# A convolution and sixteen experts in one kernel: one group's convolution sums move from TensorE to VectorE, with the loads, scatters and logits around them

## The chip, the cores and the metric

One core of a Trainium2 chip runs the whole program. The time is device microseconds of one execution, and the figure for a kernel is the median of its runs. Engines are named as in the profile: PE is TensorE (PEld its weight loads), DVE is VectorE, ACT is ScalarE, POOL is GpSimd, and SP issues most DMAs.

## What is computed

```python
# x: 8 x 2880 x 192, weight_gen: 8 x 2880 x 8 x 7
w = softmax(weight_gen, axis=-1)                         # 7 taps for each token and head
out = einsum('bshk,bskhg->bshg', w, x_unf)               # causal convolution, 8 heads x 24 channels
x = out.reshape(23040, 192)
g_logits = x @ w_group                                   # 4 groups of 4 experts
g_idx = argmax(g_logits);  g_w = softmax(g_logits)[g_idx]
e_logits = x @ w_expert[g_idx]
e_idx = argmax(e_logits);  e_w = softmax(e_logits)[e_idx]
h = relu(x @ w1[g_idx, e_idx])                           # 192 -> 1024
y = g_w * e_w * (h @ w2[g_idx, e_idx])                   # 1024 -> 192
```

Each token goes through one expert of sixteen. All of it is in 32-bit floats.

## The kernel before

The 23,040 tokens lie as 128 partitions x 180. They are taken in 15 groups of 12 columns (1,536 tokens), each in two half groups of 6.

**The front** (`front`, L656) makes, group by group, what the experts need. `load_group` (L229) loads the taps (`wt`) and the tokens (`xin`, in two parts; buffers for two groups). `softmax` (L252) is DVE with one exponential on ACT. `conv` (L274) forms the seven products of a half group on DVE (`product`, L279, `pr`, three buffers) and sums them in one of two ways. For the first `TURNED` half groups PE adds them up: nine transposes of 128 x 128 for each product accumulate in three PSUM banks (L319), and the sum comes out turned. For the others DVE adds with six additions (L298). `route` (L351) makes logits on PE (`logits`, L357: eight products for four columns, in 32 columns of the array), then the choice of expert, and the position of each token's row (`posi`, L500). A turned sum gives its logits directly and is turned back by `back` (L369, three transposes and a copy on ACT each). Another sum is first turned by `forward` (L378), three transposes and a copy into `xT` for every two columns, with logits after every second. POOL then scatters the rows of 12 x 128 tokens to the place of their expert in device memory (`scatters`, L519, L533).

**The visits.** A visit takes up to 256 rows of one expert through both products (`gemm1` L881, `gemm2` L908, LAG = 2 units behind; a visit has four units). `table` (L547) lists at the end of each round, from counts, which block and which expert each visit has; ROUNDS (L19) says that the first round ends with group 2 and has 10 small visits (128 rows, weights used as they are loaded), that round 1 has 4 visits of 256 rows, round 2 has 5, and so on for each further group. The large ones split w1 into a high and a low part (`split`, L802, cast on ACT and subtraction on DVE, both recorded as L806, L809 and L824), and so do their rows (`xlo`). The low parts of a third of w1 are made once, by `halves` (L619), with stores to device memory. `finish` (L924) scales and evacuates the result on ACT (L928), POOL sends it (`send`, L936).

**What sets the order.** PE, ACT, DVE and SP run in the order in which the program emits. `blocks` (L961) emits the visits, unit by unit, and between them steps the front (`fill`, `step`, `move`) by clocks that it keeps itself (`run`, L203). Loads are put on a list by `ask` (L977) and emitted by `pump` (L964), which stops at the first that is not ready. `ask_w` asks for w1, part 3 is w2, part 0 is the rows (`xb`, L770), which wait on the chip for the scatters. `warm` (L209) emits fillers (L214) that keep PE active. Small visits have three buffers of w1 (`wa`), four of w2 (`wc`); large ones two of raw w1. Small transposed tiles share one bank (`tp`).

```python
TURNED = 10                                                          # L25
if state["slots"] or 2 * g + n >= TURNED:                            # L288, else PE adds
if n in (2, 8) and 1 <= g < ENDS[-1] - 1:                            # L668
if end and n + 3 < n1 and (plain(n + 3) or plain(n + 1)):            # L1074
```

Of the kernel before, what the change touches and what calls it, by code (L numbers as in the profile page):

```python
# [21 lines left out]
HURRY = 12  # L22
EVERY = {}
WHOLE = (99,) * 11 + (3, 0, 0)
TURNED = 10  # L25


class Slot:
# [4 lines left out]
def conv_moe_kernel(ctx: ExitStack, tc: tile.TileContext, x, wgen, w_group, w_expert, w1, w2, out):  # L33
# [169 lines left out]
    def run(eng, cost, *deps):  # L203
        clk[eng] = max([clk[eng]] + [d + HOP for d in deps]) + cost
        return clk[eng]
# [23 lines left out]
    def load_group(g, parts=(0, 1)):  # L229
        if parts == (1,):  # L230
            s0, mid = g * SG, (SG + HALO) // 2
            nc.sync.dma_start(out=grp[g].xin[:, mid:, :], in_=xv[:, s0 - HALO + mid:s0 + SG, :])
            return
        o = grp[g] = Slot()
        o.ahead, o.chunks = False, 0
        s0 = g * SG
        o.wt = cv.tile([P, SG * H, K], F32, name="wt")
        nc.sync.dma_start(out=o.wt.rearrange("p a k -> p (a k)"), in_=wv[:, s0:s0 + SG, :])
        o.xin = cv.tile([P, SG + HALO, D], F32, name="xin")
        if s0 == 0:  # L240
            nc.gpsimd.memset(o.xin[:, 0:HALO, :], 0.0)
            nc.sync.dma_start(out=o.xin[:, HALO:, :], in_=xv[:, 0:SG, :])
            for b in range(B):
                lo, hi = b * PB, (b + 1) * PB
                nc.sync.dma_start(out=o.xin[lo + 1:hi, 0:HALO, :], in_=xv[lo:hi - 1, S - HALO:S, :])
        else:
            end = SG + HALO if 1 in parts else (SG + HALO) // 2
            nc.sync.dma_start(out=o.xin[:, 0:end, :], in_=xv[:, s0 - HALO:s0 - HALO + end, :])
# [102 lines left out]
    def route(g, o):  # L351
# [5 lines left out]
        def logits(s4, xTs):  # L357
            for u in range(2):
                for j in range(4):
                    xT, turned = xTs[j // 2]  # L360
                    if turned:
                        v, c = (((0, 0), (1, 1)), ((3, 1), (4, 2)))[j % 2][u]
                    else:
                        v, c = u * (1 + j % 2), (j % 2, 2)[u]
                    nc.tensor.matmul(  # L365
                        lt[j * LW:(j + 1) * LW, s4 // 4, :], lhsT=wr[:, v, :], rhs=xT[:, c, :],
                        start=u == 0, stop=u == 1, tile_position=(0, j * LW))
# [10 lines left out]
        def forward():  # L378
            xTs = []
            for s2 in range(0, SG, 2):  # L380
                n, i = s2 // SC, s2 % SC // 2
                if o.chunks <= n:
                    yield Chunk(o, n + 1)
                row = xrow[n][:, s2 % SC:s2 % SC + 2, :]
                if i == 0:
                    rem = rt.tile([P, SC, HP], F32, name="rem")
                    nc.scalar.copy(out=rem, in_=xrow[n][:, :, P:D])
                    txT = run("act", 0.4, clk["dve"])
                    yield NEXT
                ttp = run("pe", 0.35, txT)  # L390
                tp = ps_t.tile([P, 3, P], F32, name="tp")
                for u in range(2):
                    nc.tensor.transpose(out=tp[:, u, :], in_=row[:, u, 0:P], identity=ident)  # L393
                nc.tensor.transpose(out=tp[:, 2, :], in_=rem[:, s2 % SC:s2 % SC + 2, :].rearrange("p s d -> p (s d)"), identity=ident)
                if len(xTs) == 2:
                    run("pe", 0.5, txT)
                    logits(s2 - 4, xTs)
                    xTs = []
                xT = rt.tile([P, 3, P], F32, name="xT", bufs=2)
                nc.scalar.copy(out=xT, in_=tp)  # L400
                txT = run("act", 0.48, ttp)
                xTs.append((xT, False))
                yield NEXT
            run("pe", 0.5, txT)
            logits(SG - 4, xTs)

        turned = 2 * g < TURNED
        if turned:
# [110 lines left out]
    def scatters(g, xrow, pi):  # L519
        for s in range(SG):  # L520
            run("pool", 1.28, clk["dve"])
            scatter_row(pi[:, s:s + 1], xrow[s // SC][:, s % SC, :], round_of(g))
            yield NEXT
        if g >= MAIN and g + 1 in ENDS[:-1]:
            arrive_all(round_of(g))

# [129 lines left out]
    def front():  # L656
        side, routes = [], []
        load_group(0)
        set_up()
        load_group(1)  # L660
        yield from softmax(0)
        for g in range(ENDS[-1]):
            o = grp[g]
            routes.append([route(g, o), None])
            state["urgent"] = g == FIRST
            for n, c in enumerate(conv(g, o)):
                yield c
                if n in (2, 8) and 1 <= g < ENDS[-1] - 1:  # L668
                    load_group(g + 1, (n // 8,))
                if n >= (12 if state["slots"] else 4) and not o.ahead and g + 1 < ENDS[-1]:  # L670
                    o.ahead = True
                    side.append([softmax(g + 1), None])
                if g == FIRST - 1 and n == 4:
                    slow.append([halves(), None])
                    yield from move(slow, slow[0], 1)
                if g >= FIRST and n % 2 == 0 and not state["urgent"]:
                    for q in list(slow):
                        yield from move(slow, q, 2)
                if not state["urgent"]:
                    for q in side[:1]:  # L680
                        yield from move(side, q, 3)
                for q in spread[:1]:
                    yield from move(spread, q, 1)
                if routes:
                    yield from move(routes, routes[0], HURRY if FIRST <= g < MAIN else 3 if g < FIRST else 8 if g in ENDS else 2)
            yield from finish_all(side)
            yield from finish_all(routes, 1)
            yield from finish_all(spread, 1)
        yield from finish_all(spread)
        yield from finish_all(routes)  # L690
# [270 lines left out]
    def blocks(n0, n1, paced):  # L961
        want, jobs = [], []

        def pump(upto=None):  # L964
            for a in list(want):
# [8 lines left out]
                want.remove(a)  # L974
                load(*a)

        def ask(n, part):  # L977
            if n < n1:
                want.append((n, part))

        def ask_x(n):
# [44 lines left out]
        if n0 + 2 < n1 and plain(n0 + 2):  # L1026
            ask_w(n0 + 2)
            ask(n0 + 2, 3)
        for n in range(n0, min(n0 + 3, n1)):
            ask(n, 0)  # L1030
        if n0 + 2 < n1 and not plain(n0 + 2) and (whole(n0 + 2) or whole(n0 + 1)):
# [15 lines left out]
        for i in range(len(units) + LAG):  # L1047
            if i < len(units):
                n, j, u = units[i]
                gemm1(cur, u)  # L1050
                queue.append((cur, u))
                if i + NU - u < len(units):
                    if u == 0:
                        pump(units[i + NU][0])
                        nxt = block(i + NU)
                        prep_d(nxt)
                    if u == 1:
                        prep_x(nxt, (i + NU) // NU)
                if u == NU - 1 and i + 1 < len(units):
                    cur = nxt  # L1060
            asks = []
            if i >= LAG:
                b, u = queue.pop(0)
                gemm2(b, u)
                if u == NU - 1:
                    finish(b)
                    if i - LAG + 1 < len(units) and units[i - LAG + 1][0] != units[i - LAG][0]:
                        asks.append(units[i - LAG][0] + 3)
            if i < len(units):
                n, j, u = units[i]  # L1070
                nb = blocks_of(n)
                at = j * NU + u
                end = at == nb * NU - 1
                if end and n + 3 < n1 and (plain(n + 3) or plain(n + 1)):  # L1074
                    ask_w(n + 3)
                did = 0
                for job in list(jobs):
                    m, part, h = job
                    if m > n + 2 or (part == 3 and (m > n + 1 or at < LAG)):
                        continue  # L1080
                    must = end and m == n + 1
                    if not must and (did >= 1 or (m, part) in want or not ready(m)):
                        continue
                    jobs.remove(job)
                    work_split(job)
                    did += 1
                state["unit"] += 1
            flush()
            if paced:
                fill(clk["pe"] + AHEAD[0 if cur.plain else 1 if cur.o.whole else 2])  # L1090
            for a in asks:
                ask_x(a)
            pump()
# [40 lines left out]
```

## Time and profile before

| | us |
|---|---|
| median of 3 runs | 1240.73 (1240.4 to 1241.85) |
| the profiled execution, its own time | 1243.13 |
| its span | 1241.5 |
| PE busy in the span | 1190.0 |
| DVE busy | 922.6 |
| ACT busy | 662.1 |
| POOL busy | 428.0 |

The profile is of one execution, and sums made from its rows compare with its own time. A timeline row says when a group of like instructions starts, how long it is on record and how long its engine stood before it, with the instruction that ended this. PE's rows overlap, so what one costs is the distance to the next row's start. One product in 32-bit floats is two records in PE's rows, a transpose is one.

### The profile page before, as it was taken

Reading aid. Unit: us, or ns where it says so; the run is one execution under the profiler, and the core shown is the slowest. Engines: PE = TensorE matmul, PEld = TensorE weight load, DVE = VectorE, ACT = ScalarE, POOL = GpSimd, SP = SyncE. Lnnn points to the kernel's source line nnn. Section 1 sums busy time; section 2 is a strip of 40 time slices with the busy share of each in tenths; the row PEclk is TensorE's granted clock in tenths of the full one; section 3 lists DMA queues with packets and bytes.
Section 4 is the critical chain, followed back from the end, with each engine's and each line's share of the span. In section 5 each row is a group of like instructions: output and inputs, shape, how many; then the busy total and the mean of one; then the engine's idle time right before and its main releaser. Section 6 shows DMA issues by size and latency. Waiting matters only on the chain.

```text
span 1241.5 us, 26600 instructions
## 1 busy us (share of the span) xinstructions
PE 1190.0 (96%) x9456; PEld 1162.9 (94%) x9456; DVE 922.6 (74%) x1582; ACT 662.1 (53%) x1242; POOL 428.0 (34%) x412
## 2 busy tenths in 40 slices
PE   5998899899999999999999999999998999999995
PEld 5887899899999999999999999999998999999995
DVE  8887678698989898898899889961255776777500
ACT  1223333455565555555656565555665777777531
POOL 3062424151626253433424342444154112211111
PEclk9999999899999999999999999999998999999998
DMA  4448988888877888797969786868569777776891
GB/s 150 137 137 245 271 289 263 251 248 268 245 259 232 274 237 265 214 295 222 282 204 301 218 279 206 238 199 259 179 188 300 226 224 232 221 224 199 233 261 43
DMA packets 181677, 286.08 MB, mean 230 GB/s; under 512 B 16084, under 2 KB 141775, under 8 KB 181280
## 3 DMA queue, kind: packets, MB, share of 16 engines
q1 hardware_dynamic: 162304, 245.09, 65.8%
q0 software_dynamic: 19232, 39.22, 9.6%
q8 instruction: 76, 1.25, 0.4%
q14 instruction: 65, 0.53, 0.1%
HBM read 240.89 MB, written 44.33 MB: 230 GB/s over the span
## 4 chain that ended last, share of the span: by engine, by line
PE 67%; issue 20%; DVE 4%; POOL 4%; DMA 3%; ACT 1%; SPq 0%; POOLq 0%; DVEq 0%; ACTq 0%
PE py L919 27%; PE ph L892 27%; POOL out L936 3%; PE pl L365 2%; PE ph L319 1%; PE py L214 1%; DVE pr L280 1%; PE py L319 1%; PE tpx L319 1%; PE tpx L868 1%; PE tpx L869 1%; PE tp L393 1%; DMA raw<-in_moe_w 1%; PE tp L374 1%; DMA wc<-in_moe_w 1%
## 5 line engine op out<-in xcount | busy, mean ns | idle before, releaser
L892 PE MATMUL ph<-xh,wa 128*128 128x256 f32 x2064 | 459.7, 299 | 0.0
L936 POOL DMA_INDIRECT out<-xb x190 | 207.2, 1090 | 657.3 <-ACT xb L928 407.5
L919 PE MATMUL py<-wc,hh 128*128 128x192 f32 x2240 | 417.7, 327 | 9.8 <-ACT xb L928 9.8
L919 PEld LDWEIGHTS py<-wc,hh 128*128 128x128 f32 x2240 | 359.9, 191 | 10.2 <-ACT xb L928 10.2
L892 PE MATMUL ph<-xlo,wa 128*128 128x256 f32 x1376 | 359.4, 283 | 0.0
L892 PEld LDWEIGHTS ph<-xh,wa 128*128 128x128 f32 x2064 | 351.0, 191 | 7.4 <-issue 5.9
L898 ACT ACTIVATE hh<-ph 128x512 f32<-128x512 f32 (+1 forms) x316 | 173.2, 548 | 317.2 <-PE ph L892 317.2
L892 PEld LDWEIGHTS ph<-xlo,wa 128*128 128x128 f32 x1376 | 262.5, 191 | 0.0
L280 DVE TENSOR_TENSOR pr<-xin,wt 128x1152 f32<-128x1152 f32 x190 | 253.6, 1351 | 6.2 <-PE tpx L319 6.1
L533 POOL DMA_INDIRECT rows<-xrow,posi x180 | 201.9, 1122 | 133.2 <-DVE posi L500 57.2
L298 DVE TENSOR_TENSOR xrow<-xrow,pr 128x1152 f32<-128x1152 f32 x120 | 162.4, 1353 | 0.6
L824 DVE TENSOR_TENSOR wa<-raw,wa 128x1024 fp32r<-128x1024 f32 x86 | 104.9, 1220 | 71.2 <-ACT wa L806 63.8
L921 PE MATMUL py<-wc,hh 128*128 128x384 f32 x400 | 122.5, 362 | 0.0
L824 DVE SCALAR_TENSOR_TENSOR hl<-ph,hh 128x512 fp32r<-128x512 f32 x100 | 69.1, 691 | 66.8 <-ACT hh L903 66.4
L922 PE MATMUL py<-wc,hl 128*128 128x192 f32 x400 | 100.8, 252 | 0.0
L806 ACT CAST wa<-raw 128x1024 fp32r<-128x1024 f32 x86 | 90.3, 1050 | 6.2 <-DMA raw<-in_moe_w 6.2
L809 ACT CAST wa<-raw 128x1024 fp32r<-128x1024 f32 x86 | 89.5, 1040 | 0.0
L928 ACT ACTIVATE xb<-py,xb 128x192 f32<-128x192 f32 x190 | 71.6, 420 | 27.3 <-PE py L919 21.5
L892 PE MATMUL ph<-xd,wa 96*128 96x128 f32 x576 | 78.8, 281 | 0.5 <-ACT xd L862 0.5
L922 PEld LDWEIGHTS py<-wc,hl 128*128 128x128 f32 x400 | 77.5, 194 | 0.0
L921 PEld LDWEIGHTS py<-wc,hh 128*128 128x128 f32 x400 | 76.2, 190 | 0.0
L892 PEld LDWEIGHTS ph<-xd,wa 96*128 96x128 f32 x576 | 75.1, 198 | 0.8 <-ACT xd L862 0.7
(165 smaller groups left out, 1291.2 us busy)
## 6 DMA issues: line engine op xcount, KB each, us to landing
wc<-in_moe_w SPq DMA_DIRECT2D x79, 768.0 KB
raw<-in_moe_w SPq DMA_DIRECT2D x86, 512.0 KB
raw<-in_moe_w SPq DMA_DIRECT2D x102, 256.0 KB
xin<-in_x SPq DMA_DIRECT2D x26, 864.0 KB
raw<-w1lo SPq DMA_DIRECT2D x86, 256.0 KB
raw<-in_moe_w SPq DMA_DIRECT2D x25, 768.0 KB
xb<-rows SPq DMA_DIRECT2D x86, 194.0 KB
wa<-in_moe_w SPq DMA_DIRECT2D x36, 384.0 KB
```

Source lines behind the costliest of these rows:

```text
L280: nc.vector.tensor_tensor(out=dst, in0=o.xin[:, c0 + k:c0 + k + SC, :].rearrange("p s (h g) -> p s h g", g=HG), in1=w4[:, c0:c0 + SC, :, k ...
L298: nc.vector.tensor_tensor(out=acc, in0=acc, in1=prs[k - 2], op=ALU.add)
L533: written_once(nc.gpsimd.indirect_dma_start(out=rows[:, :], out_offset=bass.IndirectOffsetOnAxis(ap=idx, axis=0), in_=src, in_offset=None, ...
L806: nc.scalar.copy(out=o.wa[:, 0, :], in_=o.raw[0])
L809: nc.scalar.copy(out=o.wa[:, 2, :], in_=o.raw[1])
L824: f(*a, **k)
L892: nc.tensor.matmul(ph[:, v, :], lhsT=w[:, f0:f0 + P], rhs=rhs, start=i == 0, stop=i == len(terms) - 1)
L898: nc.scalar.activation(out=hh, in_=ph, func=AF.Relu)
L919: nc.tensor.matmul(b.py[t][:, 0:D], lhsT=hh[:, v, c], rhs=wc[0][:, f, :], start=f == 0, stop=f == NFT - 1)
L921: nc.tensor.matmul(b.py[t], lhsT=hh[:, v, c], rhs=wc[f // 4][:, f % 4].rearrange("p l d -> p (l d)"), start=f == 0, stop=False)
L922: nc.tensor.matmul(b.py[t][:, 0:D], lhsT=hl[:, v, c], rhs=wc[f // 4][:, f % 4, 0, :], start=False, stop=f == NFT - 1)
L936: ins = nc.gpsimd.indirect_dma_start(out=out[:, :], out_offset=bass.IndirectOffsetOnAxis(ap=b.x.bitcast(I32)[:, t, D + 1:D + 2], axis=0), ...
```

## The change

- `TURNED` is 8: group 4's two half groups are summed on DVE, and group 4 takes the way of `forward`. Groups 0 to 3 stay.
- In `forward`, groups before `BATCH` = 13 keep all six turned tiles (four in buffers of `hl`, two in `xT`) and make their 24 logits products in one go.
- `scatters`: up to group 7 the front emits two scatters for each unit, not one.
- `front`: the first part of a group's load is emitted at the first step of the group before, not the third, for groups 2 to 4.
- `blocks`: the fourth visit's w2 is asked for at the start; w1 of the first two large visits is asked for one visit earlier; nothing is asked for twice.

```diff
-TURNED = 10
+TURNED = 8
+BATCH = 13
...
-                if len(xTs) == 2:
+                if len(xTs) == 2 and g >= BATCH:
                     run("pe", 0.5, txT)
                     logits(s2 - 4, xTs)
                     xTs = []
-                xT = rt.tile([P, 3, P], F32, name="xT", bufs=2)
+                if g < BATCH and s2 < 8:
+                    xT = wp.tile([P, 3, P], F32, name="hl", bufs=4)
+                else:
+                    xT = rt.tile([P, 3, P], F32, name="xT", bufs=2)
...
-            run("pe", 0.5, txT)
-            logits(SG - 4, xTs)
+            run("pe", 0.25 * len(xTs), txT)
+            for q in range(len(xTs) // 2):
+                logits(SG - 2 * len(xTs) + 4 * q, xTs[2 * q:2 * q + 2])
...
             scatter_row(pi[:, s:s + 1], xrow[s // SC][:, s % SC, :], round_of(g))
-            yield NEXT
+            if g >= 8 or s % 2:
+                yield NEXT
...
-                if n in (2, 8) and 1 <= g < ENDS[-1] - 1:
-                    load_group(g + 1, (n // 8,))
+                at = (0 if g < FIRST + 2 else 2, 8)
+                if n in at and 1 <= g < ENDS[-1] - 1:
+                    load_group(g + 1, (at.index(n),))
...
+        asked = set()
+
         def ask(n, part):
-            if n < n1:
+            if n < n1 and (n, part) not in asked:
+                asked.add((n, part))
                 want.append((n, part))
...
             ask(n0 + 2, 3)
+            if n0 + 3 < n1 and plain(n0 + 3):
+                ask(n0 + 3, 3)
...
-                if end and n + 3 < n1 and (plain(n + 3) or plain(n + 1)):
+                if end and n + 3 < n1 and plain(n + 3):
                     ask_w(n + 3)
+                if end and n + 4 < n1 and plain(n + 2) and not plain(n + 4):
+                    ask_w(n + 4)
```

Three places where the emitted order moves. Lines behind the first edit have other numbers in the changed kernel.

PE at the first visit. `xb_158` are its rows, turned by two transposes; `ident,pr` are accumulating transposes, here the last of group 2, `pl<-hl` its logits. Before:

```order
L214 MATMUL py_1398<-ident 128x128 x9
L319 MATMUL ph_1397<-ident,pr 128x128 x3
...
L214 MATMUL py_1398<-ident 128x128 x11
L365 MATMUL pl<-hl,wr 32x128 x16
...
L860 MATMUL tp<-ident,xb_158 96x128 x2
L892 MATMUL ph_1584<-xd_167,wa 128x128 x4
```

Changed:

```order
L215 MATMUL py_1409<-ident 128x128 x13
L867 MATMUL tp<-ident,xb_158 96x128 x2
L899 MATMUL ph_1492<-xd_167,wa 128x128 x4
L320 MATMUL ph_1408<-ident,pr 128x128 x3
...
L899 MATMUL ph_1519<-xd_167,wa 128x128 x4
...
L215 MATMUL py_1409<-ident 128x128 x14
L366 MATMUL pl<-hl,wr 32x128 x16
```

The first visit's transposes and its first two units now stand ahead of the last 27 accumulating transposes of group 2 and of its logits.

SP before the large visits: `raw_170` and `raw_171` are the two buffers of w1, which visits 10 and 11 use, 12 uses the first again; `xb_160` are visit 10's rows. Before:

```order
L786 DMA raw_170<-in_moe_w 128x1024
...
L770 DMA xb_160<-rows 128x388
...
L786 DMA raw_170<-in_moe_w 128x1024
...
L786 DMA raw_171<-in_moe_w 128x1024
```

Changed:

```order
L793 DMA raw_170<-in_moe_w 128x1024
...
L777 DMA xb_159<-rows 128x194
...
L793 DMA raw_171<-in_moe_w 128x1024
...
L777 DMA xb_160<-rows 128x388
...
L793 DMA raw_170<-in_moe_w 128x1024
```

Visit 11's load stood behind visit 12's; now it stands ahead of visit 10's rows, and visit 10's ahead of visit 9's rows.

DVE at the positions of group 4 (`posi`), with the subtractions of the large visits (`wa<-raw` for w1, `xlo` for the rows). Before, where two `xlo` rows stand ahead of it in the program:

```order
L824 TENSOR_TENSOR wa<-raw_170,wa 128x1024
L824 TENSOR_TENSOR xlo<-tpx,xh_168 128x512
L497 TENSOR_REDUCE pos<-sel 128x12
L500 SCALAR_TENSOR_TENSOR posi<-pos 128x12
L558 TENSOR_TENSOR units<-cnt,per_unit 128x16
```

Changed, with six:

```order
L831 TENSOR_TENSOR wa<-raw_170,wa 128x1024
L831 TENSOR_TENSOR xlo<-tpx,xh_168 128x512
L269 TENSOR_TENSOR wt<-wt,z 128x672
...
L502 TENSOR_REDUCE pos<-sel 128x12
L505 SCALAR_TENSOR_TENSOR posi<-pos 128x12
```

For group 5 the counts are 8 and 12, for group 6 they are 14 and 17, for groups 7 to 13 two or three more than before, and for group 14 one more. The whole of PE's order has 504 accumulating transposes where it had 630, and 310 fillers where it had 325.

## Rows read from the trace of the kernel before

**Rows 1.** The page: busy time of the engines over the span, and from its list of groups the scatters of the front and the additions of the half groups that DVE sums (busy us, mean ns of one, idle before).

```profile
PE 1190.0 (96%) x9456; PEld 1162.9 (94%) x9456; DVE 922.6 (74%) x1582; ACT 662.1 (53%) x1242; POOL 428.0 (34%) x412
...
L533 POOL DMA_INDIRECT rows<-xrow,posi x180 | 201.9, 1122 | 133.2 <-DVE posi L500 57.2
L298 DVE TENSOR_TENSOR xrow<-xrow,pr 128x1152 f32<-128x1152 f32 x120 | 162.4, 1353 | 0.6
```

**Rows 2.** Windows: stretch, its length, then busy time of PE, PEld, DVE, ACT and POOL, granted clock of PE (1 is 2.4 GHz), share of time in which the DMA engines are busy, GB/s.

```profile
101.30:238.70 137.40, 122.74 (x1053) 116.23 (x1051) 98.66 (x190) 50.15 (x116) 39.10 (x34) 0.95 0.86 259
124.00:155.00 31.00, 26.52 (x203) 25.76 (x202) 20.79 (x48) 9.98 (x23) 14.31 (x12) 0.94 0.98 271
155.00:186.00 31.00, 30.01 (x282) 28.67 (x280) 22.55 (x38) 12.22 (x30) 6.96 (x6) 1.00 0.89 291
238.70:832.00 593.30, 593.30 (x4640) 579.59 (x4639) 536.96 (x882) 346.38 (x644) 243.91 (x214) 1.00 0.80 247
```

**Rows 3.** Timelines of PE, ACT, DVE and SP around 131 us, the first hole: start, us, engine, line, operation, count, and in brackets the idle time before with what ended it.

```profile
130.75 1.06 PE L892 MATMUL ph<-xd,wa 96*128 96x128 f32 x8
136.00 0.92 PE L919 MATMUL py<-wc,hh 128*128 128x192 f32 x4 [4.19 <-ACT xb L928]
...
140.27 0.82 PE L919 MATMUL py<-wc,hh 128*128 128x192 f32 x4
...
134.34 0.76 ACT L258 ACTIVATE wt<-wt 128x672 f32<-128x672 f32 x1 [5.83 <-DVE wt L257]
...
132.56 0.85 DVE L255 TENSOR_REDUCE m<-wt 128x96 f32<-128x672 f32 x1 [7.99 <-DMA wt<-in_weight_gen]
...
126.56 0.58 SPq L238 DMA_DIRECT2D wt<-in_weight_gen  x1
```

**Rows 4.** Timelines of PE, ACT and SP around 230 us, the second hole, up to the first product of a large visit (238.75).

```profile
227.92 1.05 PE L892 MATMUL ph<-xd,wa 96*128 96x128 f32 x8
234.57 1.65 PE L919 MATMUL py<-wc,hh 128*128 128x192 f32 x4 [5.59 <-ACT xb L928]
...
238.75 0.77 PE L892 MATMUL ph<-xh,wa 128*128 128x256 f32 x2
...
232.39 1.04 ACT L806 CAST wa<-raw 128x1024 fp32r<-128x1024 f32 x1 [6.17 <-DMA raw<-in_moe_w]
...
224.84 0.35 SPq L786 DMA_DIRECT2D raw<-in_moe_w  x1
```

**Rows 5.** Timeline of PE: two rows of three accumulating transposes each.

```profile
130.10 0.49 PE L319 MATMUL py<-ident,pr 128*128 128x128 f32 x3
130.43 0.49 PE L319 MATMUL tpx<-ident,pr 128*128 128x128 f32 x3
```

**Rows 6.** Timelines of POOL, SP and PE ahead of the first visit: the last scatter of group 1, the load of the first three visits' rows, then PE's fillers, logits, transposes back, and the first visit's transposes and products.

```profile
100.38 1.91 POOL L533 DMA_INDIRECT rows<-xrow,posi  x1 [0.30 <-issue]
...
107.92 3.10 SPq L770 DMA_DIRECT2D xb<-rows  x3
...
103.81 1.15 PE L214 MATMUL py<-ident 128*128 128x128 f32 x9
...
110.56 1.08 PE L365 MATMUL pl<-hl,wr 128*32 128x128 f32 x32
...
112.01 0.55 PE L374 MATMUL tp<-ident,hl 128*128 128x128 f32 x3
...
...
115.36 0.43 PE L860 MATMUL tp<-ident,xb 128*96 128x128 f32 x2 [0.57 <-ACT xrow L375]
116.24 1.99 PE L892 MATMUL ph<-xd,wa 96*128 96x128 f32 x8 [0.46 <-ACT xd L862]
```

**Rows 7.** Timeline of PE: one of the three batches of logits of group 5, between a transpose and the products of a visit.

```profile
267.84 0.27 PE L394 MATMUL tp<-ident,rem 128*128 128x128 f32 x1
268.04 0.64 PE L365 MATMUL pl<-xT,wr 128*32 128x128 f32 x16
268.62 0.50 PE L892 MATMUL ph<-xh,wa 128*128 128x256 f32 x2
```

**Rows 8.** DMA issues from 60 to 260 us: destination and source, queue, count, KB each.

```profile
wc<-in_moe_w SPq DMA_DIRECT2D x15, 768.0 KB
wa<-in_moe_w SPq DMA_DIRECT2D x20, 384.0 KB
xin<-in_x SPq DMA_DIRECT2D x8, 864.0 KB
w1lo<-raw SPq DMA_DIRECT2D x16, 256.0 KB
raw<-in_moe_w SPq DMA_DIRECT2D x14, 256.0 KB
raw<-in_moe_w SPq DMA_DIRECT2D x6, 512.0 KB
...
wt<-in_weight_gen SPq DMA_DIRECT2D x4, 336.0 KB
```

**Rows 9.** Timelines of DVE and PE: the positions of group 4 on DVE, the first use of rows of its round (the tenth large visit) on PE, and that of the next round (the sixteenth).

```profile
245.82 0.17 DVE L500 SCALAR_TENSOR_TENSOR posi<-pos 128x12 int32<-128x12 f32 x1
...
330.20 0.27 PE L868 MATMUL tpx<-ident,xb 128*128 128x128 f32 x1
...
398.38 0.27 PE L868 MATMUL tpx<-ident,xb 128*128 128x128 f32 x1
```

## The prediction

> **What bounds the kernel now.** I read the page's busy table first, then the windows, then the timelines of single engines where TensorE (PE) stands. PE is busy 96% of the span, DVE 74% [rows 1]. By stretch it is sharper: from 238.7 us to 832 us PE is busy 593.3 of 593.3 us, while DVE has 56 us free and the DMA engines a fifth [rows 2]. There every microsecond of PE work is a microsecond of time, and the stretch simply starts later or sooner. Before it, from 101.3 to 238.7 us, PE is busy 122.7 of 137.4 us. That part, where ten visits of 128 tokens run between the accumulating transposes of groups 2 to 4, holds two holes:
>
> - At 130.75 us PE issues a first product that needs 0.9 us, and its next row starts at 136.00. It waited for ScalarE's (ACT) evacuation of the previous visit; ACT stood in front of the exponential of group 4's weights, that for DVE, and DVE for the load of these weights, issued only at 126.56 [rows 3]. After it PE runs at half clock: from 136.00 to 140.27 it takes 4.27 us for what needs 2.52 later. Cost: 4.35 + 1.75 = 6.1 us.
> - At 227.92 us the same, 5.75 us: ACT waits 6.17 us for the weights of the second 256-token visit, which were issued at 224.84, behind those of the third [rows 4]. From 234.57 to 238.75 PE then takes 4.2 us for 1.8 us of products, at half clock again: 2.4 more. Cost: 8.1 us.
>
> **The change part by part.**
>
> *Eight half groups.* 14 products of group 4 are no longer summed on PE: 14 x 9 = 126 transposes at 0.109 us (three start 0.33 us apart [rows 5]): -13.7 us. The order has 310 fillers where it had 325: -1.6. Group 4's way back from the turned layout made PE wait for ACT between its four copies, as the 0.57 us ahead of 115.36 [rows 6]: four such waits, -2; the transposes that take their place stand between other products. DVE gets 12 additions more, 1.35 us each as in its other half groups [rows 1]: 16.2 us. They are covered by the 56 us that DVE has free behind 238.7 us and the 39 us before it [rows 2]; without that cover they would cost up to 16.2.
>
> *Loads sooner.* Group 4's weights are asked for two products earlier and stand before two stores and a load of 512 KB in SP's order. The weights of the first two 256-token visits are asked for one visit earlier, the second's no longer behind the third's (the second excerpt). I take both holes as gone: -6.1 and -8.1. What is late next is the DMA, below. The fourth visit's w2 (768 KB) is put in front of the first visit's rows; at some 300 GB/s that is 2.6 us.
>
> *The first visit stands earlier in PE's order*, before the last 27 transposes, the logits and the way back of group 2 (the first excerpt of the order). But its rows cannot come earlier: the last scatter of group 1 is issued at 100.38, and SP could start the load only at 107.92 [rows 6]. PE reaches the place at about 105.2, where the last 9 fillers end, and stands until about 112 (107.92, the extra load, and some 2 us to land). So the first visit starts 3.4 us sooner than at 115.36, and 9.6 us of work stand behind it that stood ahead (27 x 0.109, 14 fillers 1.5, logits 1.45, 12 transposes 1.3, and 2.4 us of waits for ACT, four of some 0.6): +6.2. Bounds: 4.7 if the rows land as now, 8 if the extra load delays the scatters as well. Half clock behind this wait is in both kernels (at 116.24 eight products are 1.99 us on record, at 130.75 they are 1.06 [rows 3, 6]).
>
> *Logits in one batch.* Eight products in 32 columns take 0.58 us to the next product's start, and the row before them holds PE 0.20 us instead of 0.11 [rows 7]; 24 in one go take 1.45 us (110.56 to 112.01 [rows 6]). Three batches come to about 2.1 us, one to 1.6: 0.5 us for each of groups 5 to 12, -4. Bounds: 0 and -5. The copies into other tiles cost ACT the same.
>
> *Scatters two a unit.* On the chip a scatter already follows the next after 0.30 us of issue [rows 6]; the order only moves sends out from between them. Nothing, as long as the rows are in time (rival below).
>
> *DMA.* Between the first visit's rows and the first 256-token product the new order still has to move what these are sized at [rows 8]: 16 stores and 8 loads of 256 KB for the split weights, 5 x 864 and 2 x 336 KB for groups 3 to 5, 14 x 384 and 7 x 768 KB for visits, 2 x 1,024 KB for the first two large ones, and 4 MB of rows, scatters and results: 28.4 MB. PE has 97 us of work there by the rows above (102.4 us of products before, less 12.0; then 2.4 us of half clock and 4.5 of waits for ACT). At 271 GB/s with a share of 0.98 the bytes need 105 us, at 291 with 0.89, that is 327 at full, 87 [rows 2]. So a wait between 0 and 10 us with what the last visit adds; I take 4, nearer to the faster row, because the small stores that fill 124 to 155 us are done by the half of it.
>
> By the Trainium skill ("DMA: Bandwidth & Descriptors", Specifications) a core's HBM limit is about 358 GB/s. By it, an estimate, the bytes need 79 us and this wait is nothing. No stretch of rows 2 comes near it, so the rows decide.
>
> **Sum**: -13.7 - 1.6 - 2 - 6.1 - 8.1 + 6.2 - 4 + 4 = -25.3 us. The profiled execution took 1243.13 us (span 1241.5), so 1217.8 for such a one; the median of the runs shown is 2.4 us lower, so **1215.5 us**. The first 256-token product would start at about 213 us instead of 238.75.
>
> **Rivals.**
>
> *A, a new hole before the first large visit.* For it: the visits that are left run 6.2 us each without transposes between them, each wants 1.57 MB, and the new order has ACT meet the exponential of group 5's weights before the evacuation that PE needs, not behind it; I find 3 us to spare there. Visit 10's rows queue behind 1 MB of visit 11's weights. Against it: no PE row before waited for these loads. If the DMA runs at 271 GB/s throughout or one hole of the kind of rows 4 (8.1 us) is back, 8 us more: 1224.
>
> *B, the DMA keeps up.* With no wait at all and the rows of the first visit as early as now: 1215.5 - 4 - 1.5 = 1210. For it the 327 GB/s. By the skill's limit above it would be so; no row shows that rate.
>
> *C, rows of a round come late: slower than before.* DVE now makes the positions of group 4 after the low halves of six large visits, not two, and of group 5 after twelve, not eight (third excerpt). Positions to first use were 84 us for group 4 [rows 9]; four visits of 11.4 us (398.38 less 330.20, six visits) come off. What is left, 39 us, must hold 12 scatters (1.12 + 0.30 each: 17 us [rows 1, 6]), their landing (5.6, from 102.3 to 107.9), the load of rows (3) and a unit ahead (3): about 7 to 10 us to spare. If they are late, ACT stands before the copy of these rows, and each such round costs one hole, 8.1 us. Ten rounds have this boundary; it decides from the fourth hole on, and five give 1256. Against it: later groups shift by two to three visits only, and one or two holes leave it at 1224 to 1232.
>
> The Trainium skill speaks for C ("SBUF — State Buffer", Who interferes with whom): a DVE instruction with two inputs in SBUF contends with a GpSimd instruction that reads SBUF, and here twelve such additions are added. If every scatter waited out one of 1.35 us, that would be 16 us more for twelve of them, past what is to spare. The trace hardly agrees: the 180 scatters take 1.12 us in the mean [rows 1], most of them beside a DVE that is busy nine tenths of the time [rows 2].
>
> *D, the change does not do what it says*, both holes stay because the loads stand behind others in the same queues: -25.3 + 14.2 = -11, 1230.
>
> **Chances.** The sum 50%, A 20%, B 15%, D 6%, C with one to three holes 3%, with more 5%, no change from effects that cancel 1%. Range: the likeliest case with its bounds is 1211 to 1220; adding B below, and A and the lower part of D above, gives **1207 to 1230**, which leaves out C, the outer part of D and what lies under B. Faster by over 0.2% (about 2.5 us, what a measurement of this kernel can tell from no change): 93%; within: 2%; slower: 5%.
>
> **What would show it.** Right: 168 rows of accumulating transposes in each bank instead of 210; no row of PE behind an evacuation for over 4 us between the first visit and the first 256-token product; that product at 209 to 216 us; one wait of 5 to 8 us ahead of the first visit's transposes, with half clock behind it; logits in rows of 24 for groups 4 to 12; PE full from there on, and the hole near 949 us, which I leave as it is, about 25 us sooner. Wrong: a wait of ACT for a load of weights or rows of over 3 us in that stretch (A, D), or PE holes behind 250 us at the start of rounds (C).

## The result and the profile after

| | before | changed |
|---|---|---|
| median of 5 runs, us | 1240.88 (1240.40 to 1241.85) | 1221.56 (1217.02 to 1223.24) |
| ratio to before | | 0.9835, interval 0.9814 to 0.9856 |
| the profiled execution, us | 1243.13 | 1217.97 |
| first 256-token product on PE, us | 238.75 | 217.91 |
| PE busy, us | 1190.0 | 1165.7 |

The change saves 1.65%, some 20 us. The runs lie in the forecast range and on the forecast side, but the median is 6 us above the point forecast and only 2.4 from rival A's 1224. The profiled execution happens to be the second fastest, so the spans of the two profiles differ by 25.1 us where the medians differ by 19.3; the experiments below say where its luck lies.

The page after, busy time and the two groups that answer to [rows 1] (busy us, mean ns, idle before):

```profile
PE 1165.7 (96%) x9315; PEld 1144.1 (94%) x9315; DVE 935.0 (77%) x1594; ACT 658.9 (54%) x1238; POOL 439.6 (36%) x412
...
L539 POOL DMA_INDIRECT rows<-xrow,posi x180 | 198.2, 1101 | 136.1 <-DVE posi L505 67.1
L299 DVE TENSOR_TENSOR xrow<-xrow,pr 128x1152 f32<-128x1152 f32 x132 | 178.6, 1353 | 0.6
```

PE has 24.3 us less to do. The 12 additions cost DVE 16.2 us as priced, and the scatters beside them did not get longer: 1.10 us, where they had 1.12. So the contention of DVE and GpSimd that the Trainium skill states ("SBUF — State Buffer", Who interferes with whom), which spoke for rival C, has no size in the scatters here. POOL's 190 sends of results did get longer, from 1.09 to 1.17 us in the mean, but not by these additions: e11 below, which has none of them, has 1.18.

Windows after, answering to [rows 2] (stretch, length, busy time of PE, PEld, DVE, ACT and POOL, PE's granted clock, DMA share, GB/s):

```profile
101.30:217.90 116.60, 102.32 (x845) 97.79 (x844) 82.55 (x158) 43.95 (x101) 35.59 (x34) 0.94 0.94 280
198.00:204.00 6.00, 0.23 (x3) 0.11 (x2) 5.93 (x5) 1.33 (x2) 4.52 (x5) 0.85 1.04 351
204.00:210.00 6.00, 6.00 (x28) 5.99 (x29) 1.43 (x2) 2.13 (x5) 4.74 (x5) 0.58 1.05 293
217.90:832.00 614.10, 614.10 (x4873) 605.68 (x4872) 562.40 (x926) 362.23 (x675) 261.88 (x220) 1.00 0.84 252
```

PE is full from its first 256-token product up to 832 us, as before. Ahead of that product the DMA engines are now nearly full (0.94, with 0.86 before; a share a little over 1 in a short stretch reads as full), and from 198 to 204 us PE is busy for 0.23 of 6 us. After that its clock is near half (0.58) for 6 us.

Timeline of PE after, ahead of the first visit ([rows 6] before), with half clock behind the wait:

```profile
103.42 1.58 PE L215 MATMUL py<-ident 128*128 128x128 f32 x13
109.99 0.60 PE L867 MATMUL tp<-ident,xb 128*96 128x128 f32 x2 [4.98 <-DMA xb<-rows]
111.05 2.08 PE L899 MATMUL ph<-xd,wa 96*128 96x128 f32 x8 [0.46 <-ACT xd L869]
112.91 0.85 PE L320 MATMUL ph<-ident,pr 128*128 128x128 f32 x3
...
120.30 1.75 PE L215 MATMUL py<-ident 128*128 128x128 f32 x14 [1.23 <-ACT xlo L326]
121.97 1.08 PE L366 MATMUL pl<-hl,wr 128*32 128x128 f32 x32
```

PE stands 5 us for the rows, where 6.8 were forecast (105.2 to 112); they come 2 us sooner (109.99), and the logits of group 2 come behind it. The transposes at 112.91 go at half clock (0.85 on record, where three take 0.49 at full).

Timelines of PE and SP after, from the loads of visit 10's weights (`raw`) to the first 256-token product; the last small visit's rows are the `xb` of 193.17:

```profile
197.06 1.06 PE L899 MATMUL ph<-xd,wa 96*128 96x128 f32 x8
203.89 0.66 PE L867 MATMUL tp<-ident,xb 128*96 128x128 f32 x2 [5.77 <-DMA xb<-rows]
205.63 1.91 PE L899 MATMUL ph<-xd,wa 96*128 96x128 f32 x8
...
217.91 0.48 PE L899 MATMUL ph<-xh,wa 128*128 128x256 f32 x2
...
189.89 0.35 SPq L793 DMA_DIRECT2D raw<-in_moe_w  x1
190.43 0.57 SPq L796 DMA_DIRECT2D raw<-in_moe_w  x1
191.19 0.50 SPq L796 DMA_DIRECT2D raw<-w1lo  x1
191.73 0.58 SPq L233 DMA_DIRECT2D xin<-in_x  x1
193.17 0.33 SPq L777 DMA_DIRECT2D xb<-rows  x1
```

The two old holes (131 and 229 us, [rows 3, 4]) are gone, and one like them is new. The rows, 97 KB, stand behind 1 MB of weights and 864 KB of tokens and land some 10 us after their issue. It costs 5.8 us and about 2.5 of half clock: 8.3.

The logits of one group after ([rows 7] before):

```profile
308.28 1.08 PE L366 MATMUL pl<-hl,wr 128*32 128x128 f32 x32
309.17 0.62 PE L366 MATMUL pl<-xT,wr 128*32 128x128 f32 x16
```

24 products take 0.89 and 0.55 us to the next row. Before, a group had three batches of 0.57, and a transpose ahead of a batch held PE 0.20 us where one ahead of a visit's product holds it 0.03, which now happens once and not three times: by these rows 0.6 us saved a group.

### The profile page after: what moved, and what is told of

It is laid out like the page before. It is cut to its first block, busy times and chain, and to the rows that moved or that the text cites. A ratio compares the mean times of both kernels' runs of the same rounds, so it can differ in the third digit from the quotient of the medians.

```text
span 1216.4 us, 26323 instructions
## 1 busy us (share of the span) xinstructions
PE 1165.7 (96%) x9315; PEld 1144.1 (94%) x9315; DVE 935.0 (77%) x1594; ACT 658.9 (54%) x1238; POOL 439.6 (36%) x412
## 4 chain that ended last, share of the span: by engine, by line
PE 83%; DVE 5%; DMA 5%; issue 3%; ACT 2%; POOL 1%; SPq 0%; POOLq 0%; DVEq 0%; ACTq 0%
PE ph L899 36%; PE py L926 29%; PE py L928 5%; PE py L929 2%; DMA raw<-in_moe_w 2%; DVE pr L281 2%; DMA xb<-rows 2%; PE pl L366 2%; PE tpx L876 1%; PE tpx L875 1%; PE tp L394 1%; PE py L215 1%; PE ph L320 1%; PE py L320 1%; PE tpx L320 1%
## 5 line engine op out<-in xcount | busy, mean ns | idle before, releaser
L943 POOL DMA_INDIRECT out<-xb x190 | 222.5, 1171 | 618.5 <-ACT xb L935 383.7
L926 PEld LDWEIGHTS py<-wc,hh 128*128 128x128 f32 x2240 | 359.7, 190 | 0.0
L281 DVE TENSOR_TENSOR pr<-xin,wt 128x1152 f32<-128x1152 f32 x188 | 251.4, 1353 | 10.7 <-PE tpx L320 10.5
L539 POOL DMA_INDIRECT rows<-xrow,posi x180 | 198.2, 1101 | 136.1 <-DVE posi L505 67.1
L299 DVE TENSOR_TENSOR xrow<-xrow,pr 128x1152 f32<-128x1152 f32 x132 | 178.6, 1353 | 0.6
L831 DVE TENSOR_TENSOR xlo<-tpx,xh 128x512 fp32r<-128x512 f32 x86 | 59.2, 688 | 28.6 <-ACT xh L880 28.3
```

Source lines behind the costliest of these rows:

```text
L281: nc.vector.tensor_tensor(out=dst, in0=o.xin[:, c0 + k:c0 + k + SC, :].rearrange("p s (h g) -> p s h g", g=HG), in1=w4[:, c0:c0 + SC, :, k ...
L299: nc.vector.tensor_tensor(out=acc, in0=acc, in1=prs[k - 2], op=ALU.add)
L539: written_once(nc.gpsimd.indirect_dma_start(out=rows[:, :], out_offset=bass.IndirectOffsetOnAxis(ap=idx, axis=0), in_=src, in_offset=None, ...
L831: f(*a, **k)
L926: nc.tensor.matmul(b.py[t][:, 0:D], lhsT=hh[:, v, c], rhs=wc[0][:, f, :], start=f == 0, stop=f == NFT - 1)
L943: ins = nc.gpsimd.indirect_dma_start(out=out[:, :], out_offset=bass.IndirectOffsetOnAxis(ap=b.x.bitcast(I32)[:, t, D + 1:D + 2], axis=0), ...
```

## The experiments

All are edits of the changed kernel except e8, which edits the kernel before. e5 to e8 ran on a chip on which the kernel before took 1376.56 us, with engines standing some 5 us about every 73 us; three of these kernels were run again elsewhere (e10 to e12), and of e5 to e8 only the ratios on that chip are used. Visits are numbered from 0, the ten small ones first: visit 10 is the first of 256 tokens, visits 74 to 79 are the round of group 13's rows, and the last round, that of group 14's rows, begins with visit 80.

**e1: logits in three batches.**

```diff
-BATCH = 13
+BATCH = 0
```

> The changed kernel with the logits of groups 4 to 12 again in three batches of eight products (BATCH = 0), all else as changed. By my term (0.5 us for each of eight groups, and group 4 is now on this way too) it is 4 to 4.5 us slower than the changed kernel: some 1225.5 us. By the rival reading of the trace after the change, where the large visits from the first 256-token product on have gained only about 2 us up to 900 us, it is 2 us slower: 1223.5. If batches cost nothing it is within 1 us.

Measured: 1241.94 us, ratio 1.0001 (0.9988 to 1.0015): 20 us slower than the changed kernel. None of the three was near. PE, then DVE, POOL and SP, of this kernel at its last round:

```profile
1007.28 0.47 PE L875 MATMUL tpx<-ident,xb 128*128 128x128 f32 x1 [17.46 <-DMA xb<-rows]
...
960.69 0.17 DVE L505 SCALAR_TENSOR_TENSOR posi<-pos 128x12 int32<-128x12 f32 x1
...
979.60 1.19 POOL L539 DMA_INDIRECT rows<-xrow,posi  x1 [0.30 <-issue]
...
1000.69 0.54 POOL L594 DMA_DIRECT2D rows<-pad  x1 [0.97 <-issue]
...
1004.74 0.34 SPq L777 DMA_DIRECT2D xb<-rows  x1
```

The positions of group 14 are made at 960.69 us (901.29 in the changed kernel), the last scatter goes out at 979.60, the pads of the round until 1001, and only then the load for which PE stands 17.5 us. In the emitted order these positions stand behind the low halves of 67 large visits, with one batch behind 62, in the kernel before behind 61. So the batch is worth its 0.6 us a group and, here, that the last round's rows are in time.

**e2: one scatter a unit.**

```diff
-            if g >= 8 or s % 2:
-                yield NEXT
+            yield NEXT
```

> The changed kernel with one scatter for each unit, as before. In the emitted order this alone puts the first visit behind the last 27 accumulating transposes and the logits of group 2 again, as in the kernel before. My term for the early place was +6.2 us (9.6 us of work behind a wait that begins 3.4 us sooner), so by it this kernel is about 6 us faster than the changed one: 1215 us. Rival: the early place is paid for by nothing, since the wait ends sooner by as much (the trace shows the first visit at 109.99 us, 5.4 us sooner): then 4 us faster at most. Second rival: two scatters a unit do pay, because the rows of later rounds come late without them: then holes of 5 to 8 us ahead of the large visits, and slower than the changed kernel.

Measured: 1216.78 us, ratio 0.9805 (0.9779 to 0.9832): some 4 us faster than the changed kernel. The first visit stands at 115.24 us with no wait for its rows, the first 256-token product at 210.63, 7.3 us sooner. The early place costs, as the first theory has it, but 4 us come out and not 6: at 310.88 us PE waits 3.1 us, where ACT stands in front of an exponential of `route` for DVE, and with the half clock behind it this trace loses 6.4 us between visits 15 and 20 that the changed kernel's first does not.

**e3: the old rule of asking.**

```diff
-                if end and n + 3 < n1 and plain(n + 3):
+                if end and n + 3 < n1 and (plain(n + 3) or plain(n + 1)):
                     ask_w(n + 3)
-                if end and n + 4 < n1 and plain(n + 2) and not plain(n + 4):
-                    ask_w(n + 4)
```

> The changed kernel with the loads of w1 for the first two 256-token visits asked for by the old rule: visit 10's one visit later, and visit 11's behind visit 12's. Theory: the new hole of 5.8 us (and 2.5 us of half clock behind it) at 198 us, where the last small visit waits for rows that lie behind 1 MB of visit 10's weights and 864 KB of tokens, goes; the old hole of 5.8 us and 2.4 us of half clock at visit 11's weights is back. One hole for another: within 2 us of the changed kernel. Rival, as the prediction priced it: the early loads take away the old hole and the new hole has other causes (the DMA engines are full): 8 us slower, 1229.

Measured: 1228.00 us, ratio 0.9886 (0.9862 to 0.9911): 6 us slower. Its PE and ACT:

```profile
205.46 1.65 PE L926 MATMUL py<-wc,hh 128*128 128x192 f32 x4 [6.04 <-ACT xb L935]
217.24 0.92 PE L926 MATMUL py<-wc,hh 128*128 128x192 f32 x4 [2.06 <-ACT xb L935]
...
203.51 1.04 ACT L813 CAST wa<-raw 128x1024 fp32r<-128x1024 f32 x1 [7.01 <-DMA raw<-in_moe_w]
215.06 1.04 ACT L813 CAST wa<-raw 128x1024 fp32r<-128x1024 f32 x1 [2.63 <-DMA raw<-in_moe_w]
```

The wait for the last small visit's rows is gone and the old kind of hole is back, now twice: ACT waits for visit 10's weights, then for visit 11's. One hole for another, and a second: the early asking of these two loads is worth 6 us, between the two theories.

**e4: visit 10's weights behind visit 9's rows.**

```diff
-                if end and n + 4 < n1 and plain(n + 2) and not plain(n + 4):
-                    ask_w(n + 4)
...
             for a in asks:
                 ask_x(a)
+                if a + 1 < n1 and plain(a - 1) and not plain(a + 1):
+                    ask_w(a + 1)
```

> The changed kernel with visit 11's weights still ahead of visit 12's, but visit 10's asked for only behind the rows and w2 of visit 9. Theory: rows behind weights make the new hole, so it goes (8.3 us) and the old one stays away: 1213 us, unless visit 10's own weights now come late, which costs a part of it back (at most the 8 us). Rival: the DMA engines are full from 186 to 218 us whatever the order, and the wait only moves to the next load: within 2 us of the changed kernel. The runs of the changed kernel lie between 1217.0 and 1223.2; if the new hole is what varies, the runs of this one lie within 2 us.

Measured: 1224.65 us, ratio 0.9865 (0.9843 to 0.9888): 3 to 4 us slower. PE stands 5.72 us at 206.31, behind an evacuation, instead of 5.77 at 203.89 behind rows; ACT stands 6.59 us in front of the cast of visit 10's weights, which are issued from 192.82 us on. So the rival's mechanism holds, though the time is a little outside its 2 us: the wait moves to the load that now stands last. Its runs spread by 8 us, no less.

**e5, e11: ten half groups on PE.**

```diff
-TURNED = 8
+TURNED = 10
```

> The changed kernel with TURNED = 10: group 4's half groups are summed by PE's accumulating transposes again, all else as changed. By my terms (13.7 + 1.6 + 2) it is 17 us slower than the changed kernel, less 12 logits and transposes of the other way that group 4 no longer takes behind the first large visit (some 3 us by the trace after): 14 us, 1235.5. Rival: with more PE work before the first large visit the loads have time to come, and the wait for the last small visit's rows (5.8 us and 2.5 of half clock) goes: then only 6 us slower, 1227.5. The trace shows which: the hole at about 215 us is there or not.

Measured there: ratio 1.0013 (0.9981 to 1.0046).

> TURNED = 10 in the changed kernel (the kernel of e5). By my terms 17 us slower than the changed kernel beside it, less some 3 us of forward transposes and logits of group 4: 14 us. Rival: the loads get time, the wait of 5.8 us and 2.5 of half clock ahead of the last small visit goes, and only 6 us are lost. The first 256-token product would be at about 232 us by the one and 226 by the other, where the changed kernel has 217.9.

Measured: 1224.42 us, ratio 0.9872 (0.9852 to 0.9893), beside 1221.90 for the changed kernel: 2.5 us, less than either theory. The first 256-token product is at 230.36 us, without the wait for the last small visit's rows: 12.5 us later than in the changed kernel's first trace and 10.5 later than in its second (e9). By the visits' first transposes it has lost 10.0 and 8.0 us at visit 70, 5.0 and nothing at visit 82. Most of what it gets back in between lies at visits 73 to 78, where the kernel before has its hole near 949 us and the changed kernel the one at 936. Its positions of group 14 are made at 878.62 us, behind 59 large visits, and its PE does not wait there. Windows of the kernel before, of the changed kernel and of e11 at these visits:

```profile
940.00:950.00 10.00, 7.55 (x57) 7.15 (x56) 3.16 (x5) 3.02 (x6) 4.91 (x9) 0.96 1.03 365
...
930.00:940.00 10.00, 8.22 (x61) 7.70 (x61) 6.34 (x22) 6.53 (x12) 4.58 (x7) 1.00 1.03 348
...
930.00:940.00 10.00, 10.00 (x80) 10.00 (x79) 6.82 (x10) 7.54 (x13) 1.94 (x2) 1.00 0.80 232
```

What differs in time is POOL's 16 pads of the last round, 194 KB each: they go out from 929 to 947 us before, from 921 to 943 in the changed kernel and from 897 to 918 in e11, ahead of these visits. In e1, whose pads go out from 983 us on, visits 73 to 78 are full too. That the pads are what fills the DMA engines in the hole is read from this coincidence; no run moves them alone.

**e6, e10: two scatters a unit from group 2 on.**

```diff
-            if g >= 8 or s % 2:
+            if g < 2 or g >= 8 or s % 2:
```

> The changed kernel with two scatters a unit only for groups 2 to 7: groups 0 and 1 take one a unit as before. In the emitted order the first visit then stands behind all of group 2's transposes, as with one a unit throughout. Theory: what one a unit gained (3.7 us by the ratios) comes from groups 0 and 1 alone, so this kernel is as fast, 1217; and the wait of 3.1 us that stood at 311 us there (ACT behind DVE before an evacuation), if it came from the later groups' scatters, goes: 1213. Rival: the gain came from the later groups, and this is 1221 as the changed kernel.

Measured there: ratio 0.9855 (0.9819 to 0.9892).

> Two scatters a unit only for groups 2 to 7 (the kernel of e6, whose chip stood still about every 72 us). By my term for the early place of the first visit (+6.2) this is 6 us faster than the changed kernel beside it, less what the wait for the last small visit's rows keeps; no PE wait over 2 us ahead of the first visit. Rival: the gain of one a unit comes from later groups, then it is as the changed kernel.

Measured: 1213.88 us, ratio 0.9778 (0.9756 to 0.9801), beside 0.9847 (0.9819 to 0.9874) for the changed kernel: 8.0 us faster, the best of all that ran. Its PE, and a window of the whole stretch:

```profile
114.08 0.55 PE L375 MATMUL tp<-ident,xlo 128*128 128x128 f32 x3 [0.57 <-ACT xrow L376]
115.20 0.43 PE L867 MATMUL tp<-ident,xb 128*96 128x128 f32 x2 [0.57 <-ACT xrow L376]
116.08 1.16 PE L899 MATMUL ph<-xd,wa 96*128 96x128 f32 x8 [0.46 <-ACT xd L869]
...
196.72 0.43 PE L867 MATMUL tp<-ident,xb 128*96 128x128 f32 x2 [3.12 <-DMA xb<-rows]
```

```profile
115.20:210.10 94.90, 88.79 (x726) 85.47 (x727) 74.00 (x144) 39.27 (x93) 38.73 (x33) 0.98 0.98 303
```

The first visit starts 5.2 us later than in the changed kernel's first trace, and from there to the first 256-token product PE needs 13.0 us less: 9.6 (the prediction's figure) for the work of group 2 that now stands ahead, the rest from half clock and waiting. This execution kept full clock at the first visit (1.16 us for eight products, not 2.08); e2's, with the same order there, did not (2.08 as well), so some 2 us of its lead are not the edit's, and the medians are to be believed. The wait for the last small visit's rows is 3.1 us, not 5.8: SP issues the 864 KB of tokens at 180.00 us in this order, ahead of the weights, and not between them and the rows. The wait of e2 at 311 us is not there: two scatters a unit for groups 2 to 7 pay, and for groups 0 and 1 they cost.

**e7, e12: the first part of a group's load at the third step.**

```diff
-                at = (0 if g < FIRST + 2 else 2, 8)
+                at = (2, 8)
```

> The changed kernel with the first part of each group's load again at the third step of the group before, for groups 2 to 4 too. By my term the first hole (ACT in front of group 4's exponential, DVE for the taps) comes back at about 130 us: 4.35 and 1.75 us, 6 us slower, 1227.5. Rival: the taps have time enough in the new order anyway, since fewer of PE's transposes stand ahead of them, or the first visit waits by itself longer: within 2 us.

Measured there: ratio 0.9953 (0.9924 to 0.9983).

> The first part of each group's load at the third step again for groups 2 to 4 too (the kernel of e7). By my term the first hole is back between 126 and 145 us, with ACT in front of the exponential of group 4's weights: 6 us slower than the changed kernel beside it. Rival: the taps are in time here anyway: within 2 us.

Measured: 1221.77 us, ratio 0.9854 (0.9830 to 0.9878): the changed kernel's time. This kernel tells nothing of the loads: its emitted order is the changed kernel's, row for row on PE, DVE and SP, with the taps ahead of the two stores. In e2, with one scatter a unit and `at` as changed, they stand there too; no run undoes both edits. So e12 serves as a third sample of the changed kernel. The difference on the chip of e7 is then what that chip did, not the edit's.

**e8: the batch alone, in the kernel before.**

```diff
+BATCH = 13
```

(with the edit of `forward` that reads it)

> The kernel before with nothing changed but the logits in one batch for groups 5 to 12. By my term 0.5 us for each of eight groups: 4 us faster than before, 1237. Rival: the batch is worth the 20 us that its removal from the changed kernel cost, then 1221; I hold that those came from the last round's rows (a wait of 17.5 us at 1007 us), which the kernel before does not have, so this rival should fail: no wait near 949 us longer than 3.3 us to win.

Measured: ratio 1.0012 (0.9984 to 1.0041) on the chip of the pauses. Not the 20 us; 4 us would have been 0.9968, outside the interval too, but PE stood there many times for other reasons. How much the batch gives in the old order stays open.

**e9: the changed kernel again.**

> The changed kernel unaltered, as the measure for the three beside it, and for a second trace of it. Expected: the ratio to before again 0.984, and again two holes between 100 and 218 us, 5 us ahead of the first visit at 110 us and 5 to 6 us ahead of the last small visit at about 204 us. Rival: the spread of its runs (1217.0 to 1223.2) is that of these two holes, then one of them is longer or shorter here by some us.

Measured: 1221.90 us, ratio 0.9847 (0.9819 to 0.9874). Same two holes, 6.8 us each; then, at visit 75, a third that its first trace has only in part:

```profile
937.89 0.33 PE L875 MATMUL tpx<-ident,xb 128*128 128x128 f32 x1 [1.74 <-DMA xb<-rows]
940.37 0.47 PE L876 MATMUL tpx<-ident,xd 128*128 128x128 f32 x1 [2.15 <-ACT xd L859]
```

The first trace stands 1.67 us at 936.04 and goes on at full clock. By the visits' first transposes e9 is 2.0 us behind it at visit 70 and 5.1 at visit 82. So these two executions differ by 2 us at the first visit's rows and 3 us at those of visit 75.

## Why the prediction held, and where its sum was off

The sum gave 1217.8 for an execution like the profiled one, which took 1217.97. That is luck twice over: terms that were off cancel, and that execution had a short wait at visit 75. By the medians the forecast was 6 us too fast. Of the named signs two were missed. The first 256-token product came at 217.91, not at 209 to 216: the 213 took the whole sum off 238.75, though the 4 us of logits lie behind that product, and without them the terms give 217.4. And the hole near 949 us came 12 us sooner and one visit later, not 25 sooner.

- **Eight half groups, -17.3.** Up to the first 256-token product PE's rows of transposes, way back, logits and fillers hold 13.7 + 3.9 + 1.45 + 0.46 us less for group 4, 0.9 more for the start of its other way, and 1.7 us less fillers: -20.3. I had priced the waits of the way back and not its 18 transposes and 24 logits products, nor the other way's some 3 us, most of which lie behind. In size the term was about right. Its worth beside the other edits was not: undone alone it costs 2.5 us (e11). 8.3 us of it come back as the wait for the last small visit's rows, which e11 does not have; 20.3 less 8.3 is 12.0, and e11's first 256-token product is 12.5 later. Another 2.5 go to the other way of group 4 up to visit 70, and between visits 70 and 82 the changed kernel loses 5 to 8 us to e11, most of it in the hole that stood near 949 us. Against the kernel before I took this hole as one that only moves, and in size it did: from visit 73 to 78 the kernel before takes 6.1 us more than e11, the changed kernel 4.2 and 7.3 in its first two traces. What I did not see is that it depends on when the front ends, and that it can be gone.
- **The early place of the first visit, +6.2.** Right in sign and about right in size: e10 undoes it by an edit to the scatters of groups 0 and 1 and gains 8.0 us. 4.4 come straight from it (9.6 us of rows less 5.2 of start), 2.7 from the shorter wait for the last rows, which I had not tied to it. The bounds were 4.7 to 8; the rows landed 2 us sooner than I took.
- **Loads sooner, -6.1 and -8.1, and the DMA, +4.** The two holes went, as forecast, and the DMA term was mis-sized: 8.3 us, near the 10 of its upper bound. e3 and e4 show why: wherever the weights stand, some load is last. e3 undoes the second hole's part alone and costs 6 us, where the terms gave 8.1 less the 4. What took the first hole away is shown only in part. The taps are issued at 122.04 us, not 126.56, and DVE still stands 5.82 us for them, up to 127.84; but group 4's exponential then runs at 131.86 without a wait for DVE, and PE does not stand. e12 shows that the edit to `at` is not needed for it; the other edits are not taken apart.
- **Logits, -4.** 0.6 us a group for the eight groups that had three batches, so -5, in rows of 32 and 16. e11, which has the batch but not the other way of group 4, bears it out: from the first 256-token product to visit 70 it needs 662.3 us where the kernel before needs 667.4. The changed kernel needs 664.8; the other 2.5 pay for the way of group 4. What I did not see is the batch's place in the planner: without it PE stands 17.5 us for the last round's rows (e1).
- **Rival A** happened in mechanism, one visit sooner than I put it: visit 9's rows stand behind 1 MB of visit 10's weights, and PE itself waits for them, not ACT. Its 1224 is closer to the median than my 1215.5; I gave it 20% because no PE row before had waited for these loads.
- **Rival C** did not happen where I put it (no wait at a round's start between 250 and 900 us, and scatters of 1.10 us), but it is the mechanism of e1 at the one boundary that I left out, the last.
- **The HBM limit of the Trainium skill** ("DMA: Bandwidth & Descriptors", Specifications). By it there would have been no wait for loads. The 6 us in which PE stands for them run at 351 GB/s, close to that limit, so the rule was nearer to what the engines can do than the 327 I worked with. That no row shows such a rate was true of [rows 2] alone: the kernel before has 365 GB/s from 940 to 950 us, the first of the windows under e11. The wait came all the same, since the bytes ahead of the rows count, not the mean.

## What to carry to other kernels

A small load that the critical engine needs pays for every byte that stands ahead of it in its queue: count them before a large load is asked for sooner. Price an edit to a planner's work also at its last deadline: in e1 the positions of the last group stand five visits further back, and nothing shows until PE stands 17.5 us for the last round's rows. Work taken from an engine is worth less than its rows where loads set the time behind it: here 20.3 us of PE's rows were worth 2.5 beside the other edits. And an edit whose purpose is plain may leave the emitted order as it was; compare the orders before running it.

## What the runs showed of the hardware

- With PE standing and loads queued, the DMA engines moved 351 GB/s over 6 us, where no stretch of [rows 2] went over 291; in half-microsecond slices from 186 to 206 us of the changed kernel the highest is 436:

```profile
GB/s 218 242 256 244 292 327 344 361 361 260 228 205 270 246 254 287 303 295 246 148 131 210 245 235 260 293 351 355 389 323 334 387 358 351 421 387 398 407 436 269
```

- On one chip the kernel before and the three kernels that also ran elsewhere were 11 to 12% slower: about every 73 us the engines stood for some 5 us while nothing that the profile shows held them, then PE went on at half clock (e5: granted clock 0.50 from 734 to 738 us, 0.68 to 744). The cause stays open.
- In the kernel before, in e2 and in e10, PE's rows from 100 to 116 us agree within 0.2 us. Behind the same short waits of 0.57 and 0.46 us the first eight products ran at half clock in the first two (1.99 and 2.08 us on record), at full clock in e10 (1.16). So which of the two levels is granted there is not set by PE's own order alone.
